# A written-out order of work replaced: single small loads between large ones, two more units turned by TensorE, shares of DVE's work given to ScalarE and GpSimd

## The chip, the cores and the metric

The kernel runs on one core of a Trainium2 chip. The metric is device time in microseconds (us). Three runs of the kernel before gave a median of 585.9 us (584.41 to 587.88). A profiled execution is a fourth run, of 584.2 us.

The core's engines are named as the profile names them: PE is TensorE (matrix products; PEld its weight loads), DVE is VectorE, ACT is ScalarE, POOL is GpSimd, SP is SyncE, which here only issues DMAs. Each engine takes its instructions in the order in which the program gives them, and waits where a datum or a buffer is not ready.

## The reference, cut to what matters

```python
# q, k, v, alpha: (4 batches, 8 heads, 768 steps, 48)
state = zeros((B, H, D, D))
for t in range(S):                                   # a decaying linear attention
    state = alpha[:, :, t, :, None] * state + einsum('bhd,bhe->bhde', k[:, :, t], v[:, :, t])
    y[:, :, t] = einsum('bhd,bhde->bhe', q[:, :, t], state)

x = y.transpose(0, 2, 1, 3).reshape(3072, 384)       # tokens x model
g = x @ w_gate                                       # (384, 1536)
val = x @ w_val
out = ((g * sigmoid(g)) * val) @ w_out               # (1536, 384)
```

The weights come as 8-byte floats and are cut to fp32 on the chip. Each fp32 operand of the feed-forward products is then split into a high part and a low part, and a product is the sum of three products of parts.

## The kernel before

**Attention, 16 units.** A unit is 192 steps (three chunks of 64) of all eight heads of one batch. Its work has short names, which the order list uses with the unit's number:

- `La`, `Lk`, `Lq` load alpha, k and q, `V` the values (`load_v`, L407: six DMAs of 48 KB in one task).
- alpha, k and q must be turned so that channels lie on partitions. Units 0 to 3 (`NPE = 4`, L25) do it on PE: `pa`/`pk`/`pq` copy a load to a wider tile (L379), `Ta`/`Tk`/`Tq` are six PE transposes each (L386), `ea`/`ek`/`cq` read the result from PSUM on ACT (L788). Units 4 to 15 do it on DVE: `tr`/`tk`/`tq` (L374).
- `G` and `f` are a backward and a forward scan over alpha on DVE (L436, L443); `mk` and `q` multiply k and q with them; `qc` copies a part of the latter (L468).
- k is turned once more: on PE with `K` and the ACT copies `kc` (L485, L491) for units 0 to 3, on DVE with `kr` (L496, eight instructions a unit) for the others.
- `S` are the scores (L516), `ma` their causal mask (L558), `B` or `Bw` the chunks' contributions to the state (L534), `ad` adds them up (L569), `de` carries the state into the next unit (L582), `vc` copies values (L472), `Y` gives the outputs (L591), which `yh` and `yl` split into high and low parts (L632, L635).
- the outputs go to the token-major tile `xT`: for units 0 and 1 by PE products `R` and copies `x` (L651, L661), for the others by `xr` (L665), ten small DMAs in one task.

**Feed-forward, 96 steps.** Two units make a block of 384 tokens; there are eight blocks and twelve slices of 128 hidden channels. Step s has `g`, nine PE products of 384 columns (L687), `sl` (Silu, ACT), `v`, nine more, `h` (their product, DVE, L702), `hh` and `hl` (high and low part of h; ACT, then DVE or GpSimd, L706, L710), and `o`, nine products into three output sums (L718). The first 24 steps take blocks 0 and 1, seven slices of each and then five, so that few weights are needed early; sums of the first part go out to memory and come back (`ot`, `os`, `pl`). From step 24 on, a block takes twelve steps in a row.

**Weights, 20 groups** (`weight_group`, L299). Three groups are single pieces of 128 x 384, sixteen are pairs, one is single. `wl` loads a group (384 KB a piece), `w..v0` to `v2` cut the 8-byte words to fp32 in three DVE passes (`single`, L142), `w..a` writes the high part (ACT, L321), `w..p` the low part (GpSimd or DVE, L325). The cut words lie in three buffers of the tag `t`. A raw group lies in the place of the next group's parts.

**Checks.** At the end a flag says whether the inputs were within the range that this path covers. For it the weights and alpha are loaded a second time and checked on ACT: `wr`/`wc` 36 times (L287, L292), `Lc`/`ck` 16 times (L425, L430). These loads use the three `t` buffers too.

**The order.** All this is issued from one string, `ORDER` (L43 to L134), in which each word is engine:task (t PE, v DVE, s ACT, g GpSimd, y SP), with the PSUM banks behind an @. The loop at L893 issues word after word; what an engine does is thus the sequence of its own words. Words ending in `*` or `+` are dummy products on PE (L759, L764: bf16 and fp32), with no use for the result. The order begins:

```
y:La0 y:wl0 y:wl1 y:Lq0 y:La1 y:Lk1 y:La2 s:pa0 y:Lk0 y:Lk2 t:3+ t:1* t:Ta0@01 v:w0v0 y:Lq1 v:w0v1 s:ea0 v:w0v2 y:V1
v:w1v0 s:w0a v:G0 s:pq0 s:pa1 t:2+ t:3* t:Tq0@01 v:f0 t:Ta1@23 y:V0 s:pk0 v:q0 g:w0p t:2+ t:Tk0@45 s:qc0 v:w1v1 s:ea1
```

Of the kernel before, what the change touches and what calls it, by code (L numbers as in the profile page):

```python
# [12 lines left out]
BF16 = mybir.dt.bfloat16  # L13
# [5 lines left out]
P = 128  # L19
# [5 lines left out]
NPE = 4  # L25
# [18 lines left out]
y:La0 y:wl0 y:wl1 y:Lq0 y:La1 y:Lk1 y:La2 s:pa0 y:Lk0 y:Lk2 t:3+ t:1* t:Ta0@01 v:w0v0 y:Lq1 v:w0v1 s:ea0 v:w0v2 y:V1  # L44
v:w1v0 s:w0a v:G0 s:pq0 s:pa1 t:2+ t:3* t:Tq0@01 v:f0 t:Ta1@23 y:V0 s:pk0 v:q0 g:w0p t:2+ t:Tk0@45 s:qc0 v:w1v1 s:ea1
v:w1v2 v:mk0 g:pq1 s:w1a g:pk1 t:2+ t:Tq1@01 v:w1p t:S0@23 y:La3 v:G1 y:Lq2 t:Tk1@45 y:wl2 t:K0.1@6 s:ek1 y:wl3 v:f1
s:kc0.1 t:3* t:K0.2@4 y:wl4 t:K0.0@5 s:vc0 y:wl5 s:kc0.2 v:mk1 s:kc0.0 y:wl6 s:pa3 v:ma0.2 g:pa2 t:2+ t:1* t:Bw0@4
s:cq1 y:wl7 v:w2v0 v:w2v1 v:w2v2 v:q1 s:w2a t:K1.2@0 y:Lk3 s:ad0.1 t:K1.0@1 v:ma0.1 g:w2p t:K1.1@3 s:ad0.0 v:ma0.0
t:Ta2@56 y:wl8 s:qc1 v:w3v0 s:ad0.2 v:w3v1 s:kc1.1 t:1+ t:Y0@24 v:de1 y:wl9 s:kc1.0 v:w4v0 s:kc1.2 t:S1@13 v:w4v1
s:vc1 v:w3v2 y:V2 s:ea2 t:Bw1@0 v:ma1.2 s:w3a v:w4v2 s:yh0.0 g:w3p s:yh0.1 v:yl0.0 t:Ta3@35 s:w4a v:yl0.1 v:ma1.1  # L50
s:ad1.1 t:R0.0@2 v:ma1.0 s:pk2 t:R0.1@4 v:w4p s:ad1.0 t:R0.2@6 s:x0.0 v:w5v0 s:ad1.2 v:w6v0 y:Lq3 v:G2 s:x0.1 t:1+
t:1* t:Tk2@01 s:pq2 y:wl10 t:Y1@24 s:x0.2 v:mk2 y:wl11 s:yh1.0 v:w6v1 t:1* t:Tq2@01 s:yh1.1 t:K2.1@6 y:V3 v:yl1.0
s:cq2 g:pk3 v:yl1.1 t:1* t:K2.0@2 s:vc2 t:K2.2@0 v:de2 t:Tk3@14 v:w5v1 s:kc2.0 s:kc2.2 t:1* t:R1.2@2 v:w5v2 s:kc2.1
# [1045 lines left out]
```

## Time and profile before

| | |
|---|---|
| median of three runs | 585.9 us (584.41 to 587.88) |
| profiled execution | 584.2 us, its span 582.4 us |
| PE busy | 558.8 us (96%), 5555 products |
| DVE busy | 408.4 us (70%) |
| ACT busy | 257.3 us (44%) |
| GpSimd busy | 126.1 us (22%) |
| DMA | 77.60 MB, 62.52 MB read from HBM |

The span is the time from the first to the last instruction of the profiled execution; the run's own time has 1.8 us more. An engine's share is an average over stages: the first 140 us, in which attention of the first units, the weights and the first steps meet, look different from the rest. A group's line gives its line in the kernel, engine and operation, output<-input, shapes and count, then busy time and mean duration of one in ns, then the idle time in front of it and what ended that. A PE product's duration overlaps the next one's, so nine products of 340 ns take about 1.6 us.

### The profile page before, as it was taken

Reading aid. Unit: us, or ns where it says so; the run is one execution under the profiler, and the core shown is the slowest. Engines: PE = TensorE matmul, PEld = TensorE weight load, DVE = VectorE, ACT = ScalarE, POOL = GpSimd, SP = SyncE. Lnnn points to the kernel's source line nnn. Section 1 sums busy time; section 2 is a strip of 40 time slices with the busy share of each in tenths; the row PEclk is TensorE's granted clock in tenths of the full one; section 3 lists DMA queues with packets and bytes.
Section 4 is the critical chain, followed back from the end, with each engine's and each line's share of the span. In section 5 each row is a group of like instructions: output and inputs, shape, how many; then the busy total and the mean of one; then the engine's idle time right before and its main releaser. Section 6 shows DMA issues by size and latency. Waiting matters only on the chain.

```text
span 582.4 us, 13799 instructions
## 1 busy us (share of the span) xinstructions
PE 558.8 (96%) x5555; PEld 529.5 (91%) x5555; DVE 408.4 (70%) x628; ACT 257.3 (44%) x596; POOL 126.1 (22%) x122
## 2 busy tenths in 40 slices
PE   8899897998999999999999999999999999999996
PEld 4677886888999999999999999999999999999995
DVE  7899999998898999939989859984962312121112
ACT  5686642342331222142326664545566565552121
POOL 5215543442323121221120101310001110001110
PEclk9999999998999999999999999999999999999999
DMA  7798955322235863336483858785543353201001
GB/s 239 238 295 235 321 134 122 90 61 66 78 97 128 197 166 91 82 74 148 106 209 121 193 169 215 205 202 155 165 110 122 89 146 94 82 0 42 1 0 43
DMA packets 95361, 77.60 MB, mean 133 GB/s; under 512 B 32832, under 2 KB 92224, under 8 KB 95296
## 3 DMA queue, kind: packets, MB, share of 16 engines
q1 hardware_dynamic: 94864, 76.12, 48.8%
q8 instruction: 44, 0.72, 0.5%
q10 hardware_dynamic: 432, 0.59, 0.3%
q14 instruction: 21, 0.17, 0.1%
HBM read 62.52 MB, written 5.90 MB: 117 GB/s over the span
## 4 chain that ended last, share of the span: by engine, by line
PE 75%; DVE 11%; DMA 8%; issue 2%; SPq 2%; ACT 0%; POOL 0%; DVEq 0%; ACTq 0%
PE ops L724 23%; PE v L692 23%; PE g L692 22%; DMA raw<-in_moe_w_out_dram 3%; DMA raw<-in_moe_w_gate_dram 2%; DVE t L151 2%; PE A L553 2%; PE s L530 2%; PE y L619 2%; DVE t L154 2%; DMA raw<-in_moe_w_val_dram 2%; DVE h L704 1%; DMA Le<-in_q_dram 1%; SPq L280 1%; DVE t L148 1%
## 5 line engine op out<-in xcount | busy, mean ns | idle before, releaser
L692 PE MATMUL v<-xT,w 128*128 128x384 f32 x864 | 168.6, 339 | 8.5 <-DVE h L704 8.5
L692 PE MATMUL g<-xT,w 128*128 128x384 f32 x864 | 167.9, 338 | 0.1
L692 PEld LDWEIGHTS v<-xT,w 128*128 128x128 f32 x864 | 151.2, 189 | 11.1 <-DVE h L704 10.3
L724 PE MATMUL ops<-w,hh 128*128 128x384 f32 x576 | 157.7, 337 | 0.0
L692 PEld LDWEIGHTS g<-xT,w 128*128 128x128 f32 x864 | 151.6, 188 | 2.0 <-ACT h L700 0.8
L704 DVE TENSOR_TENSOR h<-h,v 128x384 f32<-128x384 f32 x96 | 53.0, 552 | 102.6 <-PE v L692 100.1
L713 POOL TENSOR_TENSOR hl<-h,hh 128x384 fp32r<-128x384 f32 x54 | 57.8, 1070 | 306.1 <-ACT hh L708 295.0
L708 ACT CAST hh<-h 128x384 fp32r<-128x384 f32 x96 | 49.2, 513 | 140.2 <-DVE h L704 73.3
L724 PEld LDWEIGHTS ops<-w,hh 128*128 128x128 f32 x576 | 105.2, 188 | 0.8
L724 PE MATMUL ops<-w,hl 128*128 128x384 f32 x288 | 97.0, 337 | 1.6 <-DVE hl L713 1.5
L700 ACT ACTIVATE h<-g 128x384 f32<-128x384 f32 x96 | 47.0, 490 | 104.5 <-PE g L692 92.0
L505 DVE STREAM_TRANSPOSE K<-Gs 32x384 f32<-32x384 f32 x96 | 54.7, 570 | 2.4 <-PE A L553 0.6
L724 PEld LDWEIGHTS ops<-w,hl 128*128 128x128 f32 x288 | 54.1, 188 | 2.5 <-DVE hl L713 2.1
L713 DVE TENSOR_TENSOR hl<-h,hh 128x384 fp32r<-128x384 f32 x42 | 26.4, 629 | 26.0 <-ACT hh L708 25.5
L325 POOL TENSOR_TENSOR w<-t,w 128x768 fp32r<-128x768 f32 (+1 forms) x17 | 34.2, 2024 | 28.1 <-ACT w L321 24.8
L448 DVE TENSOR_TENSOR_SCAN AT<-AT,back 128x771 f32<-128x771 f32 x16 | 33.5, 2093 | 0.6
L563 DVE TENSOR_TENSOR X<-s,mask 64x384 f32<-64x384 f32 (+1 forms) x48 | 26.0, 554 | 9.7 <-PE s L530 7.5
L439 DVE TENSOR_TENSOR_SCAN Gs<-AT,inj 128x772 f32<-128x772 f32 x16 | 29.0, 1811 | 0.2
L464 POOL TENSOR_TENSOR X<-trq,AT 112x768 f32<-112x768 f32 x9 | 15.9, 1762 | 56.7 <-DMA xT<-X 20.7
L321 ACT CAST w<-t 128x768 fp32r<-128x768 f32 (+1 forms) x20 | 15.4, 772 | 22.2 <-DVE t L154 22.1
L297 ACT ACTIVATE wc<-wc,wbias 128x384 f32<-128x384 f32 x36 | 23.3, 648 | 1.2
L553 PE MATMUL A<-V,K 64*48 64x48 f32 (+1 forms) x720 | 21.2, 207 | 0.3 <-DVE X L563 0.3
(113 smaller groups left out, 586.1 us busy)
## 6 DMA issues: line engine op xcount, KB each, us to landing
xT<-X SPq DMA_DIRECT2D x84, 72.0 KB, 2.2
raw<-in_moe_w_gate_dram SPq DMA_DIRECT2D x12, 384.0 KB, 7.5
raw<-in_moe_w_val_dram SPq DMA_DIRECT2D x12, 384.0 KB, 7.5
V<-in_v_dram SPq DMA_DIRECT2D x96, 48.0 KB, 3.1
raw<-in_moe_w_out_dram SPq DMA_DIRECT2D x12, 384.0 KB, 7.8
wc<-in_moe_w_gate_dram SPq DMA_DIRECT2D x12, 384.0 KB, 4.4
wc<-in_moe_w_val_dram SPq DMA_DIRECT2D x12, 384.0 KB, 3.6
wc<-in_moe_w_out_dram SPq DMA_DIRECT2D x12, 384.0 KB, 4.2
```

Of the source, the lines that this page charges most:

```text
L325: eng.tensor_tensor(out=lo, in0=src, in1=hi.bitcast(F32), op=ALU.subtract)
L439: nc.vector.tensor_tensor_scan(*(x.rearrange("p g t -> p (g t)")[:, ::-1] for x in (Gs, AT, inj)), 0.0, op0=ALU.mult, op1=ALU.add)
L448: nc.vector.tensor_tensor_scan(Af, Af, back[:, 1 : n + 1], back[:, 0:1], op0=ALU.mult, op1=ALU.add)
L505: nc.vector.transpose(out=bass.AP(k0.tensor, k0.offset, [k0.ap[0], (G * 2 * D, NU), (2 * D, G), (1, 32)]), in_=Kg[j * BO + x : j * BO + x ...
L553: nc.tensor.matmul(to[j * BO : j * BO + D, g - gs.start, :], Ks[r, x, g, KC[j]], Vd[r, x, g, VC[j]], start=(x == 0 or not whole), stop=(x ...
L563: nc.vector.tensor_tensor(out=X[r, z, f * GF : (f + 1) * GF, :].rearrange("r g (c t) -> r g c t", c=NU), in0=sps[f][r].rearrange("r g (c t ...
L692: nc.tensor.matmul(pt, wsp[kind, f][a][:, kt * P : (kt + 1) * P], xT[blk][:, b_, kt, :], start=(n == 0), stop=(n == 3 * KT - 1),)
L700: nc.scalar.activation(h, acc.pop(("g", blk, f)), AF.Silu)
L704: nc.vector.tensor_tensor(out=h, in0=h, in1=acc.pop(("v", blk, f)), op=ALU.mult)
L708: nc.scalar.copy(out=hh, in_=acc["h", blk, f])
L713: eng.tensor_tensor(out=hl, in0=acc.pop(("h", blk, f)), in1=hh.bitcast(F32), op=ALU.subtract)
L724: nc.tensor.matmul(ops[blk][i], h[b_][:, i * P : (i + 1) * P], wsp["o", f][a], start=(first and n == 0), stop=(last and n == 2),)
```

## The change

- `load_v` becomes six tasks, `V{u}.0` to `V{u}.5`, one DMA each; `repack` becomes three, `xr{u}.0` to `.2`, one for each third of the channels. Number and size of the DMAs stay as they were, but for the loads of units 4 and 5.
- `NPE` is 6: units 4 and 5 are turned by PE. Each has three loads of 288 KB in place of twelve parts, three `p` copies, three `T`, three evacuations, three `K` and three `kc`, and no `tr`, `tk`, `tq`, `kr`.
- Where ACT does the first cut of a weight group (17 of 20 groups), it is one activation of the low word with a scale and a bias, and the two DVE passes behind it take other constants. The high part can be written by GpSimd (8 of 20), `qc` too (8 of 16), and `vc` (9 of 16). The low part is DVE's in 10 groups (3 before).
- For the units with `Bw`, the first chunk's and the second chunk's sums are copied together.
- The dummy products are gone; their PSUM bank `ops2` can be used by tasks.
- `weight_group` takes its pieces from `wgroups[n]`, so groups can be loaded in any order.
- `ORDER` is new as a whole. The range checks stand between step 20 and the last step (before: of the weights at steps 44 to 70, of alpha at 71 to 83).

The core of the diff:

```diff
-NPE = 4
+NPE = 6
...
+LOW = -0.93625 * 2.0 ** -51
...
-def single(nc, raw, t):
+def single(nc, raw, t, low=None):
     lo, hi = raw[:, :, 0], raw[:, :, 1]
+    if low is not None:
+        return [
+            lambda: nc.scalar.activation(t.bitcast(F32), lo, AF.Identity, bias=low, scale=LOW),
+            lambda: nc.vector.scalar_tensor_tensor(
+                out=t, in0=hi, scalar=3, in1=t, op0=ALU.logical_shift_left, op1=ALU.bitwise_or
+            ),
+            lambda: nc.vector.scalar_tensor_tensor(
+                out=t, in0=hi, scalar=0x3FFFFFFF, in1=t, op0=ALU.bitwise_or, op1=ALU.bitwise_and
+            ),
+        ]
...
-    def load_v(u, eng):
+    def load_v(u, i, eng):
         b, t0 = units[u]
         Vd = Vt[u % NV]
-        for j, r in ((0, slice(BO, BO + C)), (1, slice(0, C))):
-            for c in range(NU):
-                t1 = t0 + c * C
-                eng.dma_start(out=Vd[r, c, :, VC[j]], in_=v[b, j::2, t1 : t1 + C, :].rearrange("h s e -> s h e"))
-        if t0 == 0 and u >= NV:
+        c, j = divmod(i, 2)
+        r, t1 = slice((1 - j) * BO, (1 - j) * BO + C), t0 + c * C
+        eng.dma_start(out=Vd[r, c, :, VC[j]], in_=v[b, j::2, t1 : t1 + C, :].rearrange("h s e -> s h e"))
+        if i == 0 and t0 == 0 and u >= NV:
...
-    def repack(u):
+    def repack(u, kt, eng):
...
+            x0, x1 = max(h * D, kt * P), min((h + 1) * D, (kt + 1) * P)
+            if x0 < x1:
+                r = yrow(h) + x0 - h * D
+                eng.dma_start(
+                    out=X[x0 - kt * P : x1 - kt * P, :, kt, cs], in_=Y[r : r + x1 - x0, :, h // 2, :]
...
+        if st["whole"] and c == 0:
+            for j in range(2):
+                r = slice(j * BO, j * BO + D)
+                (eng.copy if eng is nc.scalar else eng.tensor_copy)(out=Vd[r, 1:NU, :, VC[j]], in_=st["both"][r])
+            return
...
-            if name[-1] in "*+":
-                (dummy32 if name[-1] == "+" else dummy)(int(name[:-1]))
-            else:
-                name, *banks = name.split("@")
-                todo.pop(name)(engines[e], *(BANKS[int(x)] for x in "".join(banks)))
+            name, *banks = name.split("@")
+            todo.pop(name)(engines[e], *(BANKS[int(x)] for x in "".join(banks)))
```

The new order begins, up to the first step's g0:

```
y:La0 s:pa0 t:Ta0@01 s:ea0 y:wl0 v:w0v0 v:w0v1 v:w0v2 g:w0a g:w0p y:Lq0 s:pq0 y:La1 s:pa1 t:Ta1@21 v:G0 v:f0 t:Tq0@36
v:q0 g:qc0 y:wl1 s:w1v0 v:w1v1 y:Lk0 s:pk0 t:Tk0@46 v:mk0 y:V0.0 y:V0.2 y:Lk1 s:pk1 y:Lq1 g:pq1 s:ea1 v:G1 t:Tk1@05
s:ek1 t:K0.0@1 s:kc0.0 v:w1v2 v:mk1 v:f1 t:K0.2@2 s:kc0.2 t:K0.1@3 s:kc0.1 s:w1a y:V0.3 y:wl3 s:w3v0 t:Tq1@71 s:cq1
...
v:yl0.1 g:w1p s:ad1.2 y:wl4 s:w4v0 v:w4v1 t:Ta2@12 s:ea2 v:w4v2 s:ad1.0 t:Ta3@35 v:G2 t:R0.1@4 t:R0.0@0 v:x0.0
t:R0.2@6 v:x0.2 s:x0.1 y:Lk3 y:V2.3 y:V2.0 y:Lk2 y:wl8 y:V2.1 y:wl7 y:V2.2 y:wl5 s:pk2 s:pq2 g:vc1 t:Y1@27 s:yh1.0
v:yl1.0 s:yh1.1 v:yl1.1 t:Tk2@41 t:Tq2@06 s:cq2 v:mk2 s:pk3 v:f2 v:q2 t:R1.2@2 s:x1.2 t:R1.1@7 s:x1.1 t:R1.0@6 s:x1.0
t:Tk3@04 t:K2.0@1 s:kc2.0 g:w4a g:w4p t:K2.2@7 s:kc2.2 t:K2.1@2 s:kc2.1 s:w5v0 t:g0 s:sl0 y:La4 y:Lq3 s:pq3 y:V3.4
y:V2.4 y:V3.5 y:V3.0 y:V2.5 v:de2 s:ea3 y:wl11 y:wl6 v:w5v1 s:w3a g:w3p v:w5v2 t:S2@72 t:Bw2@1 s:ad2.0 s:ad2.2 s:qc2
```

and ends:

```
t:o91 y:Lc15 s:ck15 t:v92 v:h92 s:hh92 t:g93 s:sl93 v:hl92 y:Lc4 s:ck4 t:v93 v:h93 s:hh93 g:hl93 t:g94 s:sl94 t:o92
y:Lc9 s:ck9 y:Lc12 s:ck12 t:v94 v:h94 s:hh94 v:hl94 y:wr33 s:wc33 t:g95 s:sl95 y:Lc8 s:ck8 t:v95 t:o93 v:h95 s:hh95
y:Lc13 s:ck13 v:hl95 t:o94 t:o95 v:ot95.1 s:ot95.0 s:os95.0 s:os95.1 v:ot95.2 s:os95.2
```

More of the change, by code (lines that the diff above doesn't have):

```diff
@@ L49 @@
[L49 to L53, printed above, removed]
@@ L192, in main_path @@
     inj = cp.tile([P, G, T1], F32, name="inj")
-    busy32 = inj[:, 0, 0:P]
-    busy = busy32.bitcast(BF16)
     nc.vector.memset(inj[:, 0, 0:T], 0.0)
@@ L261, in main_path @@
     HSEG = 7
-    wsp, groups, wtiles = {}, [], []
+    wsp = {}
     wlist = [("g", 0), ("v", 0)]
@@ L297, in range_check, with weight_group @@
         nc.scalar.activation(dev, dev, AF.Relu, bias=wbias, scale=-1.0, accum_out=wviol[:, 0, i : i + 1])
-    def weight_group(pieces):
-        n = len(groups)
-        groups.append(pieces)
+    def weight_group(n):
+        pieces = wgroups[n]
         size = len(pieces) * NB
@@ L315, in weight_group, with high @@
         parts = []
-        def high(src):
+        def high(eng, src):
             parts.append(p2.tile([P, 2, size], F32R, tag=f"w{n}", name=f"w{n}", bufs=1))
@@ L320, in high @@
                 wsp[piece] = tuple(parts[0][:, x, i * NB : (i + 1) * NB] for x in range(2))
-            nc.scalar.copy(out=parts[0][:, 0, :], in_=src)
+            (eng.copy if eng is nc.scalar else eng.tensor_copy)(out=parts[0][:, 0, :], in_=src)
         def low(eng, src):
@@ L327, in weight_group, with cut @@
         if is32:
-            return [], [lambda: high(raw)], [lambda eng: low(eng, raw)]
+            return [], [lambda eng: high(eng, raw)], [lambda eng: low(eng, raw)]
         raw = raw.rearrange("p (c two) -> p c two", two=2)
         t = []
-        def cut(i):
+        def cut(eng, i):
             if not i:
                 t.append(p2.tile([P, size], U32, tag="t", name=f"t{n}", bufs=NTS))
-            single(nc, raw, t[0])[i]()
+                t.append(lbias if eng is nc.scalar else None)
+            single(nc, raw, t[0], t[1])[i]()
         return (
-            [lambda i=i: cut(i) for i in range(3)],
-            [lambda: high(t[0].bitcast(F32))],
+            [lambda eng, i=i: cut(eng, i) for i in range(3)],
+            [lambda eng: high(eng, t[0].bitcast(F32))],
             [lambda eng: low(eng, t[0].bitcast(F32))],
@@ L466, in qhat, with q_odd @@
             )
-    def q_odd(u):
+    def q_odd(u, eng):
         X, r = state[u]["X"], slice(BO, BO + D)
-        nc.scalar.copy(out=X[r, 1, 0:GF, :], in_=X[r, 0, 0:GF, :])
+        (eng.copy if eng is nc.scalar else eng.tensor_copy)(out=X[r, 1, 0:GF, :], in_=X[r, 0, 0:GF, :])
     def values_copied(u, eng):
@@ L756, in main_path @@
     steps += [(blk, f, f == 0, f == NF - 1) for blk in range(2, NBLK) for f in range(NF)]
-    early_ps = ps.tile([P, 512], F32, tag="ops2", name="early_ps")
-    def dummy(n):
-        for _ in range(n):
-            nc.tensor.matmul(early_ps, busy[:, 0:P], busy.unsqueeze(1).to_broadcast([P, 2, 2 * P]), start=True, stop=True)
-    def dummy32(n):
-        for _ in range(n):
-            nc.tensor.matmul(early_ps, busy32[:, 0:P], busy32.unsqueeze(1).to_broadcast([P, 4, P]), start=True, stop=True)
     todo, turned, wfns = {}, {}, {}
@@ L774, in named_unit @@
             todo[f"L{nm}{u}"] = lambda eng, nm=nm: load_u(u, nm)
-        todo[f"V{u}"] = lambda eng: load_v(u, eng)
+        for i in range(2 * NU):
+            todo[f"V{u}.{i}"] = lambda eng, i=i: load_v(u, i, eng)
         if u < NPE:
```

198 lines of the change are left out of this document (97 added, 101 removed).

## The prediction

> **What bounds the kernel now.** I read the page first, then busy time by stage, then the chain of waits of the first 140 us, then TensorE's, ScalarE's and SyncE's own lists of instructions, and last the groups for prices. The page shows the shape:
>
> ```profile
> span 582.4 us, 13799 instructions
> PE   8899897998999999999999999999999999999996
> DVE  7899999998898999939989859984962312121112
> DMA  7798955322235863336483858785543353201001
> ```
>
> Each digit is a fortieth of the span, 14.6 us. TensorE (PE) is nearly full everywhere; VectorE (DVE) is full for the first half, and DMA only in the first 70 us. I cut the span at two events: the start of the first expert product, g0, and the end of g24, the first product of block 2, which ScalarE reads at once:
>
> ```profile
> 47.11 1.86 PE L692 MATMUL g<-xT,w 128*128 128x384 f32 x9
> 202.10 0.49 ACT L700 ACTIVATE h<-g 128x384 f32<-128x384 f32 x1 [2.69 <-PE g L692]
> ```
>
> Busy time in the three stretches (columns: us and share of PE, PE weight loads, DVE, ACT, POOL; granted clock, DMA share, GB/s):
>
> ```profile
> 0.00:47.10 47.10, 41.57 (x586) 28.27 (x586) 40.13 (x64) 32.94 (x80) 13.82 (x34) 1.00 0.85 259
> 47.10:202.10 155.00, 142.75 (x1562) 134.47 (x1562) 146.25 (x201) 56.73 (x119) 59.13 (x40) 0.99 0.53 135
> 202.10:576.60 374.50, 374.50 (x3410) 366.70 (x3408) 221.40 (x364) 167.67 (x398) 53.12 (x48) 1.00 0.44 117
> ```
>
> From 202.1 to the last product TensorE does not idle at all, and DVE is at 59%. There a shorter job on another engine is worth nothing, and every us put on TensorE costs one. In the middle stretch TensorE idles 12.25 us and DVE is busy for 146.25 of 155. What TensorE waits for there, over the whole run:
>
> ```profile
> PE v L692 <- DVE h L704: 8.5, 6, 3.5
> PE ops L724 <- DVE hl L713: 1.5, 2, 1.1
> ```
>
> That is 10.0 us of waits for DVE results, so DVE's order and load price the middle stretch. In the first stretch TensorE's 41.57 us hold much filler, and the chain there runs through weight loads that stand behind value loads on SyncE:
>
> ```profile
> 7.75 9.49 SPq L413 DMA_DIRECT2D V<-in_v_dram  x12
> 33.75 6.06 SPq L413 DMA_DIRECT2D V<-in_v_dram  x6
> ...
> 8.00:9.00 1.00, 0.79 (x4) 1.00 1.05 368
> 14.00:15.00 1.00, 1.00 (x3) 1.00 0.30 57
> ```
>
> The first two rows are SyncE issuing value loads one after another, 0.8 to 1.0 us each. The other two are single microseconds: while large loads were in flight the DMA moved 368 GB/s, and behind the twelve value loads it fell to 57. So 17 us in, the third weight piece had not been asked for.
>
> **The change, part by part.** Prices come from these groups (busy us, mean ns of one):
>
> ```profile
> L148 DVE TENSOR_SCALAR t<-raw 128x768 uint32<-128x768 uint32 x16 | 11.1, 706 | 0.1
> L151 DVE SCALAR_TENSOR_TENSOR t<-raw,t 128x768 uint32<-128x768 uint32 x16 | 17.7, 1105 | 0.4
> L325 DVE TENSOR_TENSOR w<-t,w 128x768 fp32r<-128x768 f32 x2 | 1.9, 958 | 0.0
> L374 DVE STREAM_TRANSPOSE trk<-L 128x768 f32<-128x768 f32 x12 | 19.7, 1646 | 1.3 <-POOL X L464 1.1
> L505 DVE STREAM_TRANSPOSE K<-Gs 32x384 f32<-32x384 f32 x96 | 54.7, 570 | 2.4 <-PE A L553 0.6
> L394 PE MATMUL pt<-ident,wide 128*128 128x128 f32 x72 | 10.0, 277 | 1.2 <-ACT SE L578 0.7 <-ACT wide L382 0.5
> L489 PE MATMUL kps<-ident,Gs 112*64 112x112 f32 x48 | 6.0, 260 | 0.0
> L766 PE MATMUL early_ps<-inj 128*128 128x512 f32 x28 | 14.9, 652 | 1.3 <-DVE inj L196 1.3
> L321 ACT CAST w<-t 128x768 fp32r<-128x768 f32 x16 | 13.3, 838 | 18.7 <-DVE t L154 18.7
> L382 ACT COPY wide<-Le 128x576 f32<-128x576 f32 x4 | 2.7, 672 | 4.9 <-DMA Le<-in_alpha_dram 2.1 <-DMA Le<-in_k_dram 1.9 <-DMA Le<-in_q_dram 0.8
> ```
>
> *First stretch, to g0.* I counted both order lists up to g0. DVE loses six first cuts, one of them of half width (5.5 x 0.706 = 3.9), two second cuts and one third (3 x 1.1 = 3.3), and two low parts, one of half width (1.5 x 0.958 = 1.4); a pair of decay instructions less and two copies of x more about cancel. 8.6 us less ahead of g0. ScalarE gains four first cuts (one of half width, at the price of its 768-wide pass 3.5 x 0.838 = 2.9) and three widening copies (3 x 0.672 = 2.0), and loses high parts and small copies that go to GpSimd or are joined, which I estimate at 8.4 from the counts: 3.5 us less. SyncE no longer issues twelve value loads in a row: by the list, the six of unit 0 and the six of unit 1 stand in groups of one to five between large loads, and unit 2's first waits for Y0 with five weight groups already asked for. The price of that burst is bounded by 0 (the pieces aren't needed yet) and 9.49. DVE and ScalarE are both in the chain ahead of g0, so the gain lies between 3.5 and 8.6; I take 5, nearer to the lower, since ScalarE now also waits in its order for loads: g0 near 42.
>
> *The filler goes.* All dummy products go; the 28 fp32 ones took 14.9 us, the bf16 ones less. Nearly all stand ahead of g0 where TensorE waits anyway; about 1 us lies behind g0 and is a plain gain. What they may hold up is the clock:
>
> ```profile
> 133.42 2.87 PE v L692 x9
> 136.28 2.10 PE g L692 x9
> 138.39 1.58 PE ops L724 x9
> ...
> 134.00:135.00 1.00, 1.00 (x5) 0.50 0.92 250
> ```
>
> After the 3.5 us pause, the longest wait for h above, the granted clock was 0.50 and two groups of nine products took 2.87 and 2.10 against 1.58: 1.8 us for one such pause. The order places no long pause behind g0, so I credit this 1.8 as gone and charge nothing ahead of g0; the other end is a rival below. The Trainium skill, "TensorE: Matmul & The Clock Gate", Part 1, says that the array is throttled by default and that activity releases it; its Part 4 adds that transposes count less as activity. The trace agrees on the half clock after a pause; that the first 40 us would be cold without filler, no row here shows, and it speaks against this change.
>
> *Units 4 and 5 turned by TensorE.* Each takes three turns of six transposes and three K turns of four. By busy time 72 transposes took 10.0 and 48 took 6.0, so the two units add 36 x 0.139 + 24 x 0.125 = 8.0 us to TensorE, all ahead of g24 and at full price once TensorE is the bound. ScalarE evacuates them; in the middle stretch it is at 37%.
>
> *Middle stretch, g0 to g24.* Between these marks DVE's list loses eleven first cuts (7.8), seven 32x32 turns (7 x 1.65 = 11.5) sixteen K transposes (16 x 0.57 = 9.1), together 28.4; it gains nine low parts (9 x 0.958 = 8.6), three second or third cuts (3.3), and a forward scan and some copies more against some masks less, which I estimate at 3. Net 13.5 less: 146.25 becomes 133. TensorE's becomes 142.75 + 8.0 - 1.8 - 1.0 = 148. So the order of the two turns round: DVE sat at 94% of the stretch, now at about 88% of one that TensorE fills. Idle that stays: between 0 and the old 12.25; I take 5, because first cuts on ScalarE wait in order for loads, and Silu and the high parts queue behind them, and because turns and scores now use the banks of g, v and the output sums, which the next product must wait for. 148 + 5 = 153 against 155: 2 us less.
>
> *From g24 to the end.* TensorE's work is the same. What is new is the end of ScalarE's list: range checks that stood at steps 44 to 83 now run to the last step. Rows:
>
> ```profile
> L700 ACT ACTIVATE h<-g 128x384 f32<-128x384 f32 x96 | 47.0, 490 | 104.5 <-PE g L692 92.0
> L708 ACT CAST hh<-h 128x384 fp32r<-128x384 f32 x96 | 49.2, 513 | 140.2 <-DVE h L704 73.3
> L297 ACT ACTIVATION_READ_ACCUMULATOR wc<-wc,wbias 128x1 f32 x36 | 6.8, 188 | 0.0
> L297 ACT ACTIVATE wc<-wc,wbias 128x384 f32<-128x384 f32 x36 | 23.3, 648 | 1.2
> L296 ACT ACTIVATE wc<-wc 128x384 f32<-128x384 f32 x36 | 19.8, 549 | 0.3 <-DMA wc<-in_moe_w_gate_dram 0.2
> L434 ACT ACTIVATE ac<-ac,dbias 128x576 f32<-128x576 f32 x16 | 12.4, 778 | 0.5
> wc<-in_moe_w_gate_dram SPq DMA_DIRECT2D x12, 384.0 KB, 4.4
> raw<-in_moe_w_gate_dram SPq DMA_DIRECT2D x12, 384.0 KB, 7.5
> ```
>
> With two accumulator reads of 0.19 a weight check costs 1.58; an alpha check is two passes of 0.77 and one read, 1.73. Behind sl86 stand 9 of the one and 13 of the other: 36.7 us, with ten Silu (0.49), eleven high parts (0.51) and copies 48, against 10 x 3 x 1.58 = 47.4 of products. Three buffers share the loads: 4.4 to land and 1.6 to check is a cycle of 6.0, so 2.0 per check, 22 checks in 44 us. Both just fit. Bounds: 0, and, if each load took the 7.5 us that the early ones took when the DMA was full, a cycle of 9.1, 3.0 per check, 15 checks in the densest six steps in 45.5 us against 28.4 of products, 17 more; the DMA moves little else there, so I take 1.5.
>
> **The sum**: -5 (g0) - 2 (to g24) + 1.5 (end) = -5.5. The profiled execution took 584.2 us, its span of 582.4 and 1.8 around it, which is 0.3% under the median of 585.9. That gives 578.7 on its own scale and 580.4 on the median's; I predict 579.
>
> **The rivals.** *TensorE stays full* (faster still). If g0 comes the whole 8.5 earlier and idle falls to 1, the parts are -8.5, -6 and 0: 585.9 - 14.5 = 571. For it: DVE's lists are shorter at every mark. Against: three engines would have to meet without a wait.
>
> *The relief comes back as waits* (no change). SyncE's list puts the loads of groups 8, 7 and 5 behind value loads that wait for Y0, and groups 11, 6 and 10 behind Y1; ScalarE's first cuts queue before Silu. If idle in the middle stays at 12.25 and g0 gains only 3.5, the parts are -3.5, +5 and +1.5: near 589 at worst, 586 with half of it.
>
> *The clock stays at half until g0* (slower). TensorE has about 25 us of useful work ahead of g0 (the 41.57 less the 14.9 and the bf16 filler). At half clock that is 25 more; with the weight loads out of the way, the turns, carries and outputs of units 0 and 1 join the chain. With half of it there, 12.5 against the 5.5 gained: 593. It decides from about 5.5 us of lost clock, three pauses as priced above.
>
> **How the numbers follow.** A measurement of this kernel can tell about 0.5% from no change: faster is under 583.0, slower over 588.8. Forecast (574 to 583) 0.44; TensorE full (568 to 574) 0.17; relief returned (583 to 588.8) 0.21; slower, the clock 0.11 and the crowded end or a blocked queue 0.07. Faster 0.61, same 0.21, slower 0.18. The range leaves out the last us of either side: 568 to 590; the forecast's own is 574 to 583.
>
> **What would show it.** Right: g0 at 40 to 44; the end of g24 at 192 to 198 with idle of TensorE under 8 us between; DVE under 140 us busy there; no idle of TensorE from g24 to step 85, and at most 2 us behind it; 45 fewer dummies with the clock at 1.00 in most of the first 40 us. Wrong: a clock of 0.50 over ten or more of them with g0 past 47; TensorE waits on ScalarE casts or loads between g0 and g24 of over 10 us; or Silu of steps 86 to 95 late behind its checks.

## The result, and the profile after

The changed kernel takes 567.4 us (median, 567.05 to 569.77), the kernel before 585.8 on the same chip: a ratio of 0.969 with a 95% interval of 0.965 to 0.973. The gain of 18.4 us has the sign that was forecast and about three times the size; 567.4 lies just under the range of 568 to 590. The profiled execution of after took 567.05 us, its span 565.3.

The page of after, the rows that answer to those shown of before:

```profile
span 565.3 us, 13806 instructions
PE   4799999999999999999999999999999999999996
DVE  7789898988798996775897778867574632121113
DMA  8977556565244652653133566265261142516552
```

TensorE is full from the third slice on. The valley in the DMA row of before, 32223 in its eighth to twelfth slice, is filled but for a 2 in the eleventh. The busy times of after by stage, cut at the same events, g0's start, g24's end and, within 0.2 us, the last expert product (columns: length in us, then busy us, with instructions, of PE, its weight loads, DVE, ACT, POOL; granted clock, DMA share, GB/s):

```profile
0.00:40.90 40.90, 29.11 (x546) 26.11 (x547) 32.02 (x52) 29.35 (x65) 23.76 (x40) 0.96 0.85 244
40.90:182.28 141.38, 140.60 (x1547) 137.03 (x1545) 122.96 (x183) 72.78 (x150) 51.79 (x42) 1.00 0.54 152
182.28:560.80 378.52, 375.47 (x3480) 368.10 (x3478) 221.42 (x366) 156.88 (x378) 74.97 (x73) 1.00 0.44 116
```

The first stretch is 6.2 us shorter (40.9 for 47.1), the middle 13.6 (141.4 for 155.0); the last is 4.0 longer (378.5 for 374.5), and behind the last product stand 4.5 us in place of 5.8. Together 17.1, the difference of the two spans.

The second busy time of each row, that of the weight loads, tells where the 13.6 went. Before, TensorE loaded weights for 134.47 of 155.00 us, so for 20.5 us it loaded none; after, for 137.03 of 141.38, a gap of 4.35. The load grew by 2.6, the gaps shrank by 16.2. Busy time shows 11.5 of these 16.2 as idle (12.25 before, 0.78 after) and hides the other 4.7: it read 142.75 before, 8.3 us without a weight load among it, and 3.6 after. A small rest is no waiting: in the last stretch of before, where TensorE never idles, weight loads leave 7.8 of 374.5 us, about 2%. The Trainium skill, "Perfetto Trace Analysis", section "Identifying the Most-Contended Engine", says that matmul busy time is a poor measure since matmuls are pipelined, and that the share of weight loads is a better one; these two traces agree, but for that 2%.

TensorE's waits over the whole run of after:

```profile
PE pt L415 <- ACT wide L403: 8.1, 3, 5.2
PE A L574 <- issue: 3.1, 2, 2.8
PE A L574 <- DMA V<-in_v_dram: 2.3, 2, 1.4
...
PE v L714 <- DVE h L726: 0.2, 1, 0.2
```

The 8.5 for h and 1.5 for hl are gone. What is left lies ahead of g0 (nearly all of the first two rows) or in the last stretch (the third, two value loads that come late).

### The profile page after: what moved, and what is told of

Read it like the earlier page. It is cut to its first block, busy times and chain, and to the rows that moved or that the text cites. A ratio compares the mean times of both kernels' runs of the same rounds, so it can differ in the third digit from the quotient of the medians.

```text
span 565.3 us, 13806 instructions
## 1 busy us (share of the span) xinstructions
PE 545.4 (96%) x5570; PEld 531.3 (94%) x5570; DVE 377.0 (67%) x601; ACT 259.0 (46%) x591; POOL 150.5 (27%) x155
## 4 chain that ended last, share of the span: by engine, by line
PE 84%; DMA 5%; SPq 4%; ACT 3%; DVE 2%; issue 1%; DVEq 0%; ACTq 0%
PE g L714 25%; PE v L714 25%; PE ops L746 24%; PE A L574 2%; DMA V<-in_v_dram 2%; PE y L645 2%; PE pt L415 2%; PE s L550 1%; DMA L<-in_k_dram 1%; PE y L628 1%; SPq L699 1%; PE y L629 1%; SPq L433 1%; PE kps L509 1%; DMA raw<-in_moe_w_gate_dram 1%
## 5 line engine op out<-in xcount | busy, mean ns | idle before, releaser
L735 POOL TENSOR_TENSOR hl<-h,hh 128x384 fp32r<-128x384 f32 x55 | 62.5, 1137 | 268.2 <-ACT hh L730 266.0
L525 DVE STREAM_TRANSPOSE K<-Gs 32x384 f32<-32x384 f32 x80 | 45.6, 570 | 5.6 <-PE A L574 2.7
L735 DVE TENSOR_TENSOR hl<-h,hh 128x384 fp32r<-128x384 f32 x41 | 25.6, 627 | 23.9 <-ACT hh L730 23.7
L468 DVE TENSOR_TENSOR_SCAN AT<-AT,back 128x771 f32<-128x771 f32 x16 | 30.5, 1906 | 0.6
L574 PE MATMUL A<-V,K 64*48 64x48 f32 (+1 forms) x720 | 22.5, 209 | 5.3 <-issue 3.1
L415 PE MATMUL pt<-ident,wide 128*128 128x128 f32 x108 | 18.5, 326 | 8.4 <-ACT wide L403 8.1
L574 PEld LDWEIGHTS A<-V,K 64*48 64x48 f32 (+1 forms) x720 | 20.0, 125 | 6.0 <-issue 3.3
L415 PEld LDWEIGHTS pt<-ident,wide 128*128 128x128 f32 x108 | 15.4, 170 | 10.2 <-POOL sel L369 5.2
```

The source lines that it names most:

```text
L415: nc.tensor.transpose(pt[:, j - js.start, :], Wd.rearrange("p j e c -> p (j e c)")[:, j * P : (j + 1) * P], ident)
L468: nc.vector.tensor_tensor_scan(Af, Af, back[:, 1 : n + 1], back[:, 0:1], op0=ALU.mult, op1=ALU.add)
L525: nc.vector.transpose(out=bass.AP(k0.tensor, k0.offset, [k0.ap[0], (G * 2 * D, NU), (2 * D, G), (1, 32)]), in_=Kg[j * BO + x : j * BO + x ...
L574: nc.tensor.matmul(to[j * BO : j * BO + D, g - gs.start, :], Ks[r, x, g, KC[j]], Vd[r, x, g, VC[j]], start=(x == 0 or not whole), stop=(x ...
L735: eng.tensor_tensor(out=hl, in0=acc.pop(("h", blk, f)), in1=hh.bitcast(F32), op=ALU.subtract)
```

## The experiments

All medians stand beside a run of the kernel before on the same chip (584.5 to 586.2), and the ratios are to that. "In the trace" compares the time of one Silu with that of the same Silu in after, or in before where the old order is meant.

### One part undone in the new order

**e1_cuts_dve**: the first cuts back on VectorE (17 words of the order).

```
-s:w3v0 ... s:w4v0 ... s:w19v0
+v:w3v0 ... v:w4v0 ... v:w19v0
```

> The kernel after, with the 17 first cuts of the weights that ScalarE makes given back to VectorE at the same places of the order; nothing else. Theory D (the gain between g0 and g24 is VectorE's relief): VectorE gets 17 passes, 11 to 12 us at the 0.706 of before's row, some 9 of them between g0 and g24, so its 123.0 busy us of 141.4 become about 132, 93% as before the change; waits of TensorE for h and hl come back, g24 ends 5 to 10 us later, and the run takes 572 to 578 against 567. Rival O (the new order and the loads' places are the gain, whoever cuts): ScalarE was at half load, VectorE still has slack, and the run stays within 2 us of 567. Rival G (the low parts moved from GpSimd): the same as O.

Measured: 571.0 us, ratio 0.977 (0.974 to 0.980). In the trace g0 stays (40.85) and g24 ends 4.4 later. Its middle stretch:

```profile
40.85:186.66 145.81, 142.47 (x1547) 136.75 (x1545) 132.40 (x197) 61.32 (x135) 50.12 (x42) 1.00 0.52 148
```

VectorE is at 132.4, as worked out, and gaps are 9.1 in place of 4.35. The first cuts are worth some 4 us, less than theory D's 5 to 10 and the 572 to 578 that it gave, and what comes late is weights (2.4 of waits on w), hardly h (0.4).

**e2_low_gp**: ten low parts of weights back on GpSimd.

```
-v:w5p ... v:w18p
+g:w5p ... g:w18p
```

> The kernel after, with the ten low parts of weights that VectorE makes behind g0 given to GpSimd at the same places. Rival G (GpSimd's two-input passes slow VectorE while both run): VectorE loses 10 passes of 0.96, but its second and third cuts go from 0.96 back to 1.10 to 1.15 and its scans from about 1.9 toward 2.3; GpSimd gets some 20 us; waits for h or for weights come back and the run takes 569 to 574. Theory D: VectorE is lighter by up to 9 us, so the run stays at 567 or gains 1, unless a low part on GpSimd comes late for its product.

Measured: 570.9, ratio 0.977 (0.974 to 0.980); g24 ends 2.7 later, and a further us goes by the end. VectorE lost ten passes of about 1.0 and yet is busy for 121.75 of its middle stretch, only 1.2 less than in after. The second and third cut of the weights in e2, and then in after:

```profile
L163 DVE SCALAR_TENSOR_TENSOR t<-raw,t 128x768 uint32<-128x768 uint32 x15 | 16.4, 1103 | 0.3
L160 DVE SCALAR_TENSOR_TENSOR t<-raw,t 128x768 uint32<-128x768 uint32 x15 | 15.3, 1018 | 4.6 <-ACT t L159 4.1 <-POOL U L495 0.3
```

```profile
L164 DVE SCALAR_TENSOR_TENSOR t<-raw,t 128x768 uint32<-128x768 uint32 x15 | 14.3, 967 | 0.3
L161 DVE SCALAR_TENSOR_TENSOR t<-raw,t 128x768 uint32<-128x768 uint32 x15 | 14.3, 954 | 4.1 <-ACT t L160 4.0
```

The same passes take 14% and 7% longer on average while GpSimd makes the low parts at 2.16 each. It isn't that all are slower: four of the 30 took 1.34 to 2.46, each beside a two-input pass of GpSimd, and the others 0.91 to 1.03, though a few of these had such a neighbour too. The longest and its neighbour (start, us, instruction):

```profile
58.22 2.46 DVE L163 SCALAR_TENSOR_TENSOR t<-raw,t 128x768 uint32<-128x768 uint32 x1
57.34 2.52 POOL L344 TENSOR_TENSOR w<-t,w 128x768 fp32r<-128x768 f32 x1
```

TensorE now waits for these low parts. What its weight loads waited for in e2's middle stretch:

```profile
PEld g L713 <- POOL w L344: 1.3, 1, 1.3
PEld ops L745 <- POOL w L344: 1.1, 2, 0.8
PEld v L713 <- POOL w L344: 0.8, 1, 0.8
```

So both held: GpSimd holds single passes of VectorE up, and its low parts come late.

**e4_turn_dve**: units 4 and 5 turned by VectorE.

```
-NPE = 6
+NPE = 4
-s:pa4 t:Ta4@06 s:ea4 ... s:pk4 t:Tk4@50 s:ek4 ... t:K4.1@0 s:kc4.1
+v:tr4 y:Lq4 ... v:tk4 y:La5 ... v:kr4.0 v:kr4.1
```

> The kernel after, with units 4 and 5 turned by VectorE again (six 32x32 turns and sixteen key turns at the places where ScalarE evacuated; the loads of these units move behind the turn that frees their buffer). Theory D (VectorE's relief): VectorE's 123.0 of the 141.4 us between g0 and g24 grow by 6 x 1.65 and 16 x 0.57, to about 142, TensorE gives 5.8 back; VectorE is the bound there again and g24 ends 5 to 12 us later, 572 to 579 against 567.4. Rival O (the places of the loads make the gain): VectorE's slack of 18 us takes it, and the run stays within 2 us of 567.

Measured: 597.6, ratio 1.023 (1.017 to 1.029), 30 us over after and more than any theory gave. Its middle stretch and TensorE's waits there:

```profile
41.73:210.38 168.65, 147.78 (x1487) 142.59 (x1485) 141.28 (x205) 62.55 (x123) 44.58 (x38) 0.92 0.51 140
```

```profile
PE v L712 <- DVE h L724: 4.8, 2, 4.0
PE A L572 <- DVE K L523: 4.1, 2, 2.3
PE ops L744 <- DVE w L343: 3.8, 2, 3.5
PE A L572 <- DVE t L162: 3.4, 1, 3.4
```

VectorE is at 141 as worked out, and TensorE idles 20.9 us, on h, keys, weights and cuts alike. The mean clock of 0.92 shows the rest: after five of these pauses it was granted at half for 27 us in all. That multiplier was in no expectation. The edit also moves loads of these units behind the turn that frees their buffer, so not all of the 30 us need be VectorE's load.

**e5_shares_back**: e1, e2 and e4 together.

> The kernel after, with all three shares undone together: the 17 first cuts and the turns of units 4 and 5 back on VectorE, ten low parts back on GpSimd. What is left of the change is the order, the single value loads and the small copies. Theory D: the three undo most of the 14 us that were gained between g0 and g24, so 578 to 586. Rival O: the order and the loads hold most of the gain, so 569 to 576. If the parts simply add up, the two that were measured alone (3.6 and 3.5) and the turns' 5 to 12 give 579 to 586.

Measured: 598.5, ratio 1.025 (1.018 to 1.031). The parts don't add: 3.6, 3.5 and 30.2 alone, 31.1 together. The turns alone cost nearly all of it; that the other two hide in the same pauses fits this, but no run takes them apart.

### The value loads

**e3_v_burst**: the six value loads of each unit where the first one stands.

```
-y:V4.1 ... y:V4.3 ... y:V4.4 y:V4.2 ... y:V4.0 ... y:V4.5
+y:V4.0 y:V4.2 y:V4.4 y:V4.1 y:V4.3 y:V4.5
```

> The kernel after, with the six value loads of each unit issued one after another where the first of them stands now; nothing else moves. Rival O (the loads' places): behind the first burst the second and third weight group are asked for 2 to 4 us later, g0 comes at 43 to 47 in place of 40.9, and the bursts of units 4 and 5 hold weight groups back while SyncE waits for the outputs of the unit two before; the run takes 571 to 577. Theory D: g0 moves by 0 to 2 and TensorE between g0 and g24 stays without idle, so the run takes 567 to 569.

Measured: 588.3, ratio 1.007 (1.005 to 1.010). The whole gain is gone, though g0 comes only 1.9 later; neither theory gave so much. **f1_burst_early** and **f2_burst_late** are the same edit for units 0 to 5 and for units 6 to 15 alone.

> The kernel after, with the value loads of units 0 to 5 alone in bursts of six (where the first of each stands); units 6 to 15 keep their single loads. The run with all bursts lost 1.9 us to the first Silu, 8.1 by step 10, 4 at step 22 and 8.8 between steps 50 and 70. If the loss is SyncE's queue (each burst holds the loads behind it 0.6 to 0.9 us a piece, and a wait for the outputs of the unit two before holds all six), the two halves add up: 574 to 577 here, 8 over 567. If a single pause anywhere lets the rest slip, this run loses all 20 and the other none.

> The kernel after, with the value loads of units 6 to 15 alone in bursts of six; units 0 to 5 keep their single loads. If the two halves add up: 4 at step 22 and 6 to 9 between steps 50 and 70, where the alpha loads that VectorE's next turn waits for stand behind four more value loads; 577 to 581. If the late loss only came of the early one: 567 to 569.

Measured: f1 575.9, ratio 0.983 (0.980 to 0.986); f2 580.9, ratio 0.992 (0.989 to 0.995). In the trace they lose 8.5 and 16.2 to the last Silu, e3 20.9: both halves count, they add up but for 4, and each loses at places of its own. (The profiled f2 is its slowest run; by medians f1 loses 8.5, f2 13.5 and e3 20.9, which add up within 1.1.) One of f1's, as SyncE, ScalarE and TensorE tell it (start, us, instruction, idle time ahead of it and what ended that):

```profile
55.60 4.91 SPq L432 DMA_DIRECT2D V<-in_v_dram  x6
...
61.73 0.62 SPq L442 DMA_DIRECT2D L<-in_k_dram  x1
```

```profile
66.67 0.67 ACT L402 COPY wide<-L 128x576 f32<-128x576 f32 x1 [6.48 <-DMA L<-in_k_dram]
```

```profile
70.62 1.54 PE L414 MATMUL pt<-ident,wide 128*128 128x128 f32 x6 [3.84 <-ACT wide L402]
```

SyncE waited 6.0 us for the outputs of unit 2 before it could issue the burst of unit 4, and unit 4's key load stood behind it; meanwhile, from 55 to 62 us, the DMA was busy for 0.27 of the time. In after that load was asked for 5.6 us sooner:

```profile
56.12 0.63 SPq L443 DMA_DIRECT2D L<-in_k_dram  x1
```

```profile
62.32 0.68 ACT L403 COPY wide<-L 128x576 f32<-128x576 f32 x1 [3.46 <-DMA L<-in_k_dram]
```

f2 has the same late in the run, where DMA is at 0.43: four value loads more ahead of an alpha load, VectorE waits 6.79 for it (2.29 in after), h stands behind that in VectorE's line, and TensorE waits 4.63 and then runs at half clock (nine products in 3.25).

```profile
425.68 1.54 DVE L394 STREAM_TRANSPOSE AT<-L 128x768 f32<-128x768 f32 x1 [6.79 <-DMA L<-in_alpha_dram]
```

```profile
428.11 3.25 PE L713 MATMUL v<-xT,w 128*128 128x384 f32 x9 [4.63 <-DVE h L725]
```

So it is SyncE's line, not the DMA's bandwidth, that the single loads relieve: each value load costs it 0.6 us or more (4.91 for the six above), and a burst takes its first wait for all six.

### Parts in the old order

**b1_no_dummy**: before without its dummy products (18 words of the order).

> The kernel before, without its 45 dummy products and nothing else. If filler keeps the clock up (the slower rival of the prediction): the granted clock is 0.50 over ten us or more ahead of g0, g0 comes past 47.1 and the run takes 588 to 598. If it doesn't matter: g0 stays at 46 to 48, the 2.0 us of dummies behind g0 go where TensorE isn't waiting, and the run takes 584 to 586 against 585.8.

Measured: 590.1, ratio 1.008 (1.005 to 1.010). Two stretches of b1, and the same of before:

```profile
30.00:35.00 5.00, 1.21 (x59) 1.01 (x51) 3.94 (x6) 4.14 (x9) 1.84 (x1) 0.82 1.07 365
35.00:40.00 5.00, 5.00 (x90) 4.91 (x90) 2.48 (x5) 0.66 (x3) 0.00 (x0) 0.50 1.00 286
```

```profile
30.00:35.00 5.00, 4.94 (x207) 4.51 (x202) 4.70 (x8) 4.87 (x13) 1.01 (x1) 1.00 1.08 364
35.00:40.00 5.00, 4.04 (x31) 2.50 (x33) 4.94 (x7) 4.81 (x14) 0.82 (x1) 1.00 1.10 322
```

Without filler g0 comes at 52.5 for 47.1, and 13.7 us ahead of it are at half clock, none in before. Not all of the loss begins with the clock. The idle time of b1's first row is one pause, which ends before the 345th product of TensorE's list:

```profile
34.88 1.60 PE L553 MATMUL A<-V,K 128*48 128x48 f32 x34 [3.79 <-issue]
```

That is where after stops as well, to load code (shown with the last runs below). So in the old order the clock rival is real, but the filler covers two things, half clock and a wait for code, and this run doesn't take them apart. The new order has the same 546 products ahead of g0 (586 before, 40 of them filler), done by 40.9, and is at 0.96 there without filler.

**b2_cuts_act**: before with the same 17 first cuts on ScalarE. **b3_v_single**: before with the value loads of units 0 and 1 in ones and twos. **b4_turn_pe**: before with units 4 and 5 turned by TensorE. **b5_all_shares**: b2, b4 and the ten low parts on VectorE. **b6_shares_singles**: b5 and b3.

```
-v:w3v0                      b2
+s:w3v0
-y:V1 y:V0 y:La3 y:Lq2       b3
+y:V0.0 y:V0.2 y:La3 y:V0.4 y:V0.1 y:Lq2 y:V0.3 y:V0.5
-v:tr4 ... v:kr4.1           b4
+s:pa4 t:Ta4@01 s:ea4 ... t:K4.0@0 s:kc4.0
```

> The kernel before, with the same 17 first cuts made by ScalarE, at the places of the order where VectorE made them; nothing else. Theory D: VectorE loses 11 to 12 us, about 8 of them in the middle stretch, and the 10.0 us of waits for h and hl fall by half or more; 577 to 582 against 585. Rival O: the old order holds VectorE at other places (loads that come late, turns), a first cut on ScalarE waits in line for its load and Silu behind it; 584 to 587.

> The kernel before, with the twelve value loads of units 0 and 1 no longer in one burst but in ones and twos between the large loads of the same list (unit 0's between key, alpha and query loads, unit 1's between weight groups 2 to 5). Rival O: the third to sixth weight group are asked for 3 to 6 us sooner, DMA no longer falls to 57 GB/s at 14 us, g0 comes at 42 to 45 in place of 47, and the run takes 579 to 583 against 585. Theory D: g0 moves by less than 1 us, since VectorE and ScalarE are what it waits for, and the run stays at 584 to 586.

> The kernel before, with units 4 and 5 turned by TensorE and evacuated by ScalarE, at the places of the order where VectorE turned them (two of the turns up to 13 words later, where banks are free), and weight group 18 loaded behind the last of them, whose buffer it shares; nothing else. Theory D (VectorE's relief is the gain, in any order): VectorE loses 19 of its 146.25 us between g0 and g24, TensorE gets 5.8; the waits for h of 8.5 fall to 2 or less, and the run takes 575 to 581 against 585. Rival F (the order and the shares only work together): VectorE's waits move to the evacuations on ScalarE and to other h's, and the run is within 2 us of 585 or over it.

> The kernel before, with all three shares of the change together: 17 first cuts on ScalarE, units 4 and 5 turned by TensorE, ten low parts on VectorE; the old order, the value bursts and the dummies stay. Theory D: most of the middle's 14 us come, 570 to 577. Rival F: the old order gives less than a third of it, 580 to 590; then the 18 us are the order's and the loads', made possible by the shares.

> The kernel before, with everything that the change does except its order: first cuts on ScalarE, units 4 and 5 turned by TensorE, ten low parts on VectorE, and the value loads of units 0 and 1 in ones and twos between the large loads. If the parts added up, 594.8 (the three shares) and 2.9 more for the loads: 597. Theory F (shares and loads pay only in an order made for them): over 585 as well, 588 to 598. Theory D: under 580.

Measured: b2 588.2, ratio 1.006 (1.003 to 1.009); b3 587.4, 1.005 (1.003 to 1.008); b4 588.5, 1.005 (1.002 to 1.008); b5 594.8, 1.017 (1.013 to 1.020); b6 596.1, 1.017 (1.013 to 1.020). All are slower than before, by 0.5 to 1.7%, and theory D falls: at the old places VectorE's relief is no gain. In b3 neither theory held: g0 came 2.4 later, not sooner. b4's middle stretch shows why the relief is lost, and with it what VectorE then waited for, and last the first row of that list in before:

```profile
47.17:206.54 159.37, 150.21 (x1622) 141.94 (x1622) 123.15 (x179) 69.89 (x150) 55.98 (x41) 0.98 0.44 121
```

```profile
DVE h L706 <- PE v L694: 14.1, 9, 5.2
DVE X L565 <- PE s L532: 7.4, 2, 6.4
```

```profile
DVE h L704 <- PE v L692: 1.7, 3, 0.9
```

VectorE falls from 146 to 123, and no wait of TensorE for h is left. But TensorE's weight loads grow by 7.5 (the turns, and longer loads at half clock, 6.83 us of it for 3.41) and its gaps only shrink from 20.5 to 17.4: it now waits for evacuations and copies on ScalarE and VectorE, in many pieces of 0.3 to 1.5. In b2, g0 comes 5.1 later, and TensorE waits ahead of it 2.8 and 1.9 for copies of the first carries, which ScalarE makes in line with the first cuts (1.9 and 0.7 in before); 6.8 us ahead of g0 are at half clock besides.

| | old order | new order |
|---|---|---|
| shares as before | 585.8 | e5: 598.5 |
| shares as after | b5: 594.8, b6: 596.1 | 567.4; with bursts (e3) 588.3 |

In these runs neither the shares nor the order gains without the other. The table is coarse: b5 and b6 keep the filler, leave out the high parts and copies that GpSimd took, and have 13 low parts on VectorE for after's 10, and e5 keeps GpSimd's copies. It compares the places that were run, not every order that the shares could have.

### What is left in the new order

**e6_loads_early** and **e7_late_v**: loads moved ahead of others.

```
-y:xr8.0 ... y:La11 v:kr9.2 y:V9.0        e7 (and V12.4, V12.1 likewise)
+y:V9.0 ... y:xr8.0 ... y:La11 v:kr9.2
-y:wl2 v:w2v0 ... y:V1.5                  e6, beside e7's
+y:V1.5 y:wl2 v:w2v0 ... s:ad1.2 s:ad1.0
```

> The kernel after, with five moves: weight group 2 asked for behind the last value load of unit 1 (TensorE waited 2.84 for that load at 24 us and then ran at half clock for 3 us); the copies of unit 1's carry ahead of a first cut and an evacuation on ScalarE; and one value load of unit 9 and two of unit 12 ahead of repacking loads (0.90 and 1.35 of waits at 257 and 346 us). If these waits are on the path: g0 1.5 to 4 us earlier, 2 us less behind it, 562 to 565 against 567.4. Rival: the wait at 24 us is only traded for the next (scores, evacuations), g0 moves by under 1, and the run takes 565 to 567.

> The kernel after, with only the three late value loads moved: one of unit 9, two of unit 12, ahead of the repacking loads. The waits of 0.90 and 1.35 go: 565 to 566 against 567.4. Rival: the repacking or alpha loads that they pass come late in turn, 567 or over.

Measured: e6 568.8, ratio 0.972 (0.967 to 0.976); e7 566.6, 0.969 (0.965 to 0.973). In both the waits for late value loads are gone from the list, but e7 can't be told from after, and in e6 the pause at 24 us is 3.45 in place of 2.84 though the value loads left sooner. g0 differs by 0.9 between e7 and after, whose lists are the same that far, so less than a us there tells nothing. The pause was misread: it isn't a value load. Around it, in after:

```profile
23.47 0.66 PE L574 MATMUL A<-V,K 128*48 128x48 f32 x20
26.97 0.88 PE L574 MATMUL A<-V,K 128*48 128x48 f32 x27 [2.84 <-issue]
```

In all ten runs whose list for TensorE is the same up to there (after, e1 to e7, f1, f2) it stands before the same product, the 345th of the list, and in b1, with another order, before the 345th too. **f3_code_shift**, **g1_shift_small** and **g2_shift_late_v** (g1 with e7's moves) put 80 products at the head of that list.

```
+    for _ in range(80):
+        nc.tensor.matmul(early_ps, busy[:, 0:P], busy[:, 0:16], start=True, stop=True)
```

> The kernel after, with 40 small products (128 rows, 64 columns) at the head of TensorE's list, where it waits 5 us anyway; they write a bank that nothing reads. In six runs that share TensorE's list the pause at 24 us stood before the 21st product of unit 1's carry, and it ended 1.3 to 1.5 us after a 16 KB packet of the instruction queue had landed. If TensorE waits there for its code, the pause moves 40 products forward in the list, into unit 1's scores, at about 23 us, and is as long or shorter; the run stays within 1.5 us of 567. If it waits for a value load or for VectorE's decay, it stays before the 21st product of the carry.

> The kernel after, with 80 tiny products (bf16, 16 columns, into a bank that nothing reads) at the head of TensorE's list, in place of the 80 slower ones of the last trial, which ended at 7.8 us and held the first turn up by 2.2. If TensorE waits for code in pages of 128 products, the pause moves 48 products back in the list, as in that trial, to the 44th of the last 48 of unit 1's carry, and shrinks from 2.84 to about 1.1; the tiny ones are done before the first turn at 5.2, so g0 comes 1 to 2 us earlier and the run takes 565 to 567 against 567.4. Rival: 80 products take over 4 us at the start here too and delay the first turn; 568 to 570.

> The same, with the three late value loads of units 9 and 12 also moved ahead of the repacking loads (alone they took the waits at 257 and 346 us away). The two are far apart in time, so their gains add: 1 to 2 for the code and 1 for the loads, 564 to 566. If either is only noise of the start (where g0 differs by up to 1 us between runs of one order), 566 to 567.

Measured: f3 570.4, ratio 0.972 (0.968 to 0.976); g1 570.3, 0.975 (0.972 to 0.977); g2 567.9, 0.970 (0.967 to 0.972). All three took longer than the main forecast of each. In all three the pause came 48 products of the kernel later, before the 473rd of the list. In f3 each of the 40 fp32 products is issued twice, so 80 stand in its list, not the 40 on which its expectation reckoned. f3's rows:

```profile
27.24 0.65 PE L574 MATMUL s<-V,K 128*48 128x48 f32 x19
29.02 0.29 PE L574 MATMUL s<-V,K 128*48 128x48 f32 x4 [1.13 <-issue]
```

The 80 added ones and these 48 are 128 products, 256 instructions with their weight loads. A 16 KB packet of the instruction queue landed at 25.54 in after, 27.48 in f3, 27.41 in g1 and 27.16 in g2; the products went on 1.4, 1.5, 1.4 and 1.5 us behind it (in b1 it landed at 33.40, and they went on 1.5 behind it). In after's DMA list for 24.5 to 25.6 us that is one packet beside a full data queue:

```profile
q1 hardware_dynamic: 470, 0.35, 100.1%
q8 instruction: 1, 0.02, 5.5%
```

TensorE waits for its code. The Trainium skill, "Runtime: NRT & Kernel Launch", section "Instruction fetch mechanics", says that code comes in blocks of 16 KB, 256 instructions, and that crossing one is mostly hidden; the traces agree on the block, and where small products meet a full DMA it isn't hidden here. The shorter pause that was expected came in f3 alone (1.13); it was 3.60 in g1 and 3.34 in g2. In before the 128 products up to that place took 7.6 us, filler among them, and there is no pause; in after they took 2.7. No version here is faster than the changed kernel by more than its interval.

## Why the prediction was wrong in size

**First stretch.** Five us were forecast, g0 near 42; it is 6.2 and 40.9. The size was right, the reason is not shown, so call it luck: the largest part of VectorE's relief was the first cuts, and with these back on VectorE (e1), or all three shares undone (e5), g0 stays at 40.8. Bursts cost g0 1.3 to 1.9 (f1, e3), but f2, whose start is that of after, has 1.1 too. Over 4 us lie in the new order of units 0 and 1, with the copies that GpSimd took, and which part of it stays open.

**The filler.** Right for the change, wrong in the reasoning: nothing was charged ahead of g0 since TensorE "waits anyway". In the old order g0 comes 5.4 later without it (b1). In after one pause of 2.84 and one stretch of half clock of 3.41 us are left there; what filler would gain was not run.

**Middle stretch, g0 to g24: the step that failed.** It said "142.75 + 8.0 - 1.8 - 1.0 = 148", 5 of idle, 153. Measured: 140.60 and 0.78, so 141.4, and 11.6 less. Four terms make that up.

The idle that stays, 4.2: it rested on queues on ScalarE and on shared banks, and the middle shows one wait, 0.8.

The first term, 3.5: it took busy time for work. With what the turns cost, without the output group of unit 6 (both below) and with the prediction's own 1.8 and 1.0, it gives 142.75 + 5.8 - 1.7 - 1.8 - 1.0 = 144.1, and 140.6 came. A row of before tells where that lay:

```profile
L692 PEld LDWEIGHTS v<-xT,w 128*128 128x128 f32 x864 | 151.2, 189 | 11.1 <-DVE h L704 10.3
```

Weight loads stood still for 10.3 us for h where products waited 8.5 in six waits: at each, the last product counts as busy for some 0.3 us more while nothing new is loaded. Such time goes with the wait.

The added term, 2.2. The turns of unit 4 in after:

```profile
82.44 0.55 PE L509 MATMUL kps<-ident,Gs 112*64 112x112 f32 x4
82.82 0.82 PE L415 MATMUL pt<-ident,wide 128*128 128x128 f32 x6
83.40 1.83 PE L714 MATMUL v<-xT,w 128*128 128x384 f32 x9
```

From start to start, four key turns take 0.38 and six transposes 0.58; six of each for the two units are 5.8, not 8.0.

The outputs of unit 6, 1.7: they stand ahead of g24 before and behind it in after. The sum had no term for that; the middle gains it and the last stretch pays it.

VectorE's 133 became 123. About half of this is the price of the second and third cuts, taken from a mean that held passes slowed beside GpSimd: between the marks 27 took 29.7 us before and 30 took 28.5 after, 1.2 less, where 3.3 more was reckoned. The scans and copies, put at 3 more, came out some 4 less; six turns went, not seven, and ten low parts came, not nine, which goes the other way.

**From g24 to the end.** 1.5 was forecast for the range checks. They cost nothing: from the Silu of step 85 to the last expert product TensorE is busy all the time, with ScalarE at 44 of 52 us.

```profile
508.95:560.61 51.66, 51.66 (x297) 51.33 (x295) 10.85 (x25) 44.03 (x104) 5.06 (x5) 1.00 0.53 154
```

The 4.0 that were lost in the last stretch are the 1.7 of unit 6, so "TensorE's work is the same" was wrong, and 2.25 for two late value loads, which the prediction didn't see.

**The rivals.** "TensorE stays full" (571) is what happened, held at 0.17 because "three engines would have to meet without a wait"; its idle of 1 was right, and its middle, 6 us shorter for the measured 13.6, still fell short by the other three terms. "The relief comes back as waits" is what the old order does with the same shares (b4, b5). "The clock stays at half" is, in part, what the old order does without filler (b1).

**What stays open.** The order was changed as one piece. That it and the shares need each other is shown for the places that were run; which of its moves closes which gap is not.

## What to carry to other kernels

For TensorE, take work from the weight loads of a stretch and call the rest gap, even where it reads as busy, but for the 2% that a full stretch leaves; at half clock weight loads grow too (140.62 in e3's middle for after's 137.03, same products). A list of work and the shares of its engines are one design: judge a share in the order made for it, since the same share in another order can cost what it would have gained. Small loads that wait for buffers belong one by one between the others, because the line that issues them waits with them, and a pause of TensorE costs more than itself: the pauses of 3.66 (e3) and 4.63 (f2) at the same alpha load lost 6.2 and 6.4 us, the rest in half clock.

## What the runs showed of the hardware

**Half clock comes in pieces of 3.41 us.** In all runs each stretch of it ahead of the last product is 3.41, 6.83 or 10.24 long. The one of after lay from 27.87 to 31.28 and began 0.9 us after TensorE had gone on; f1's of 6.83, two pieces, began 0.6 ahead of that (the number ahead of the DMA share is the granted clock):

```profile
27.87:31.28 3.41, 3.41 (x57) 3.32 (x52) 2.04 (x4) 0.63 (x3) 0.38 (x1) 0.50 1.06 324
```

```profile
70.04:76.87 6.83, 6.25 (x86) 5.66 (x87) 3.57 (x7) 4.50 (x9) 1.91 (x2) 0.50 0.13 51
```

**Code loads can stop TensorE**, for 1.1 to 3.8 us, in the runs in which the 128 products ahead of the place took 2.6 to 4.7 us while DMA moved some 220 to 370 GB/s.

**A two-input pass of GpSimd can hold one of VectorE's up for most of its length**: 2.46 us for a cut that takes 0.95, beside a low part of 2.52 (e2). Before has four such cuts among 32, of 1.65 to 2.65; after has none over 1.07.
